# Pooled attention and two feed-forward layers: GpSimd takes other low parts in the first pair, and tile 11 in the others

## The chip, the cores and the metric

The kernel runs on one core of a Trainium2 chip. The metric is the device time of one execution in microseconds (us). A core has TensorE (PE; its weight loads are listed as PEld), VectorE (DVE), ScalarE (ACT), GpSimd (POOL) and SyncE (SP), which issues the DMAs here. Each engine works through its own queue in order; semaphores tie the queues together.

## The reference

Three stages follow one another. Attention over 4 batches and 8 heads, 1152 keys of 64 values; the queries are averaged by twos, so there are 576 of them. Then two feed-forward layers over 2304 tokens.

```python
q_pool = q.reshape(B, H, S // 2, 2, D).mean(axis=3)
scores = scale * np.matmul(q_pool, k.transpose(0, 1, 3, 2))
scores = scores - np.max(scores, axis=-1, keepdims=True)
attn = np.exp(scores)
attn = attn / (np.sum(attn, axis=-1, keepdims=True) + 1e-09)
x = np.matmul(attn, v)             # heads side by side: 2304 x 512
...
h = x @ w_in;  x = (h - np.tanh(h)) @ w_out
h = x @ w_in2; y = (h * (1.0 / (1.0 + np.exp(-1.702 * h)))) @ w_out2
```

## The kernel before

Matmuls run in a rounded format (fp32r). To keep fp32 accuracy an operand is split into a high part (a copy in fp32r) and a low part (the difference), and products of high and low parts are added up in PSUM. The low parts are subtractions with two inputs in SBUF; which engine makes them, VectorE or GpSimd, is what this change is about.

Heads go in pairs, 16 pairs. A pair has 18 tiles of 128 keys, nine for each of its heads; `g` counts tiles over all pairs and `g % 18` is called the tile's number below. For each tile the loop issues, in this order: `scores(g)` (four matmuls into one of two PSUM tiles `ps_sc`, then ScalarE's exponential `pf` and, for two tiles of three, a second one that gives the high part `ph`); one or two tiles of maxima for the next pair (`max_tile`: two matmuls and one reduction on VectorE, L327 and L331; their PSUM `ps_mx` has one buffer from tile 3 on); `rest(g - 1)`, the subtraction that gives the low part `pl` of the tile before (L457); `pv(g - 3)`, the products with V of the tile three back; and then what the tables `plan` and, for pair 0, `opening` list for this tile. An entry `(o, i)` runs in tile `i` for the pair `o` places further on. Tiles 1, 4, 7 of each head have no low part: there the full fp32 product is taken.

`pool_sub` says in which tiles the subtraction goes to GpSimd; all the others go to VectorE. `sum_q` makes `qs`, the pooled queries; `prep_qh` and `prep_ql` split them; `prep_kh` and `prep_kl` split K in two halves (L303 on ScalarE, L307 on GpSimd); `prep_v_split` splits V (L416, L419); `stack` copies the split parts by six DMAs into the layout for the scores (L315 to L320; L317 carries K's low part); `max_rows` turns the maxima of a head into the row that is subtracted (a small minimum L390 and a transpose L392 on VectorE). `kl` has one buffer: a new K low part can be written only when L317 of the pair before has read the old one. In pairs 8 to 14 weights of the first layer are converted beside attention, with steps on VectorE in tiles 6, 8, 11 and 15 (L138, L144, L151, L158) in five of these pairs.

Ahead of the loop stands the opening: loads, the splits of pair 0, and the maxima of its first head (`first_max`), which all must be known before the first exponential. `keep_warm` issues matmuls on zeros so that PE does not stand still, and `scores` issues some more in tiles 1 to 3. In PSUM, `ps_first` (two buffers of three banks) lies behind `ps_sc[0]`; when it closes, the second scores tile `ps_sc[1]` and `ps_two` (two buffers of maxima, up to tile 3) take its room.

Of the kernel before, what the change touches and what calls it, by code (L numbers as in the profile page):

```python
# [7 lines left out]
F32 = mybir.dt.float32  # L8
# [3 lines left out]
ALU = mybir.AluOpType  # L12
AX = mybir.AxisListType
# [15 lines left out]
def tile_pooled_attention_two_moe(  # L29
# [182 lines left out]
    def attention(ctx: ExitStack):  # L212
# [22 lines left out]
        def refill_v(i, n):  # L235
            old, new = [(*vt[x], vfs[x])[n] for x in (0, i)]
            nc.scalar.activation(new[:, :, D:128], old[:, :, D:128], AF.Copy)

        def refill_row(i):
            row = [stacks[x][1][D:D + 1, :] for x in (0, i)]  # L240
            nc.scalar.activation(row[1], row[0], AF.Copy)
# [21 lines left out]
        def load_k(p, rows=slice(0, 128)):  # L263
            if p not in kraw:
                kraw[p] = ap.tile([128, S], F32, tag="kr", name="kr", bufs=2)
            nc.sync.dma_start(out=kraw[p][rows], in_=k[p // NPB, p % NPB][rows])

        def load_v(p, s):
            vraw[p, s] = ap.tile([128, 2 * KG, D], F32, tag=f"vr{s}", name=f"vr{s}")
            nc.sync.dma_start(out=vraw[p, s], in_=v[p // NPB, p % NPB][:, s, 0:2 * KG])  # L270
# [11 lines left out]
        def sum_q(p, eng=nc.vector):  # L282
            eng.tensor_add(pairs[p]["qs"], qraw[p][:, 0], qraw[p][:, 1])
# [17 lines left out]
        def prep_kh(p, x):  # L301
            xs = slice(x * SP, (x + 1) * SP)
            nc.scalar.activation(pairs[p]["kh"][:, xs], kraw[p][:, xs], AF.Copy)  # L303
# [7 lines left out]
        def stack(p, s):  # L311
            d = pairs[p]
            a1, a2, q2, q3 = stacks[(2 * p + s) % 3]
            r = slice(64 * s, 64 * s + 64)
            nc.sync.dma_start(out=f32(a1[0:64, :]), in_=f32(d["kh"][r, :]))  # L315
            nc.sync.dma_start(out=f32(q2[0:64, :]), in_=f32(d["qh"][r, :]))
            nc.sync.dma_start(out=f32(a1[64:128, :]), in_=f32(d["kl"][r, :]))  # L317
            nc.sync.dma_start(out=f32(q2[64:128, :]), in_=f32(d["qh"][r, :]))
            nc.sync.dma_start(out=f32(a2[0:64, :]), in_=f32(d["kh"][r, :]))
            nc.sync.dma_start(out=f32(q3[0:64, :]), in_=f32(d["ql"][r, :]))  # L320
# [16 lines left out]
        def first_max(s, j, x, pool, parts, n, banks=2):  # L337
            d = pairs[0]
            a1, _, q2, _ = stacks[0]
            r = slice(64 * s, 64 * s + 64)  # L340
            lhs, rhs = (q2, a1) if s == 0 else (d["qh"], d["kh"])
            mx = pool.tile([128, banks, 512], F32, tag="mx", name="mx")
            if j < 4:
                for a in range(parts):
                    k0 = (x * parts + a) * n
                    nc.tensor.matmul(
                        mx[:, a, 0:n], lhs[r, 128 * j:128 * j + 128], rhs[r, k0:k0 + n],
                        start=True, stop=True)
            else:
                for a in range(parts):  # L350
                    for h in range(2):
                        q0, k0 = 512 + 64 * s - 64 * h, h * SP + a * n
                        nc.tensor.matmul(
                            mx[:, a, 0:n], bdqs[1][r, q0:q0 + 128], rhs[r, k0:k0 + n],
                            start=(h == 0), stop=(h == 1))
            c = 64 + 16 * x + 5 * s + j
            nc.vector.tensor_reduce(
                first_mt[:, c:c + 1], mx[:, 0:parts, 0:n], AX.XY, ALU.max, negate=True)

        def row_part(s, row, j):  # L360
            c = 5 * s + j
# [46 lines left out]
        def prep_v(p, s):  # L408
            prep_v_whole(p, s)
            prep_v_split(p, s)  # L410
# [12 lines left out]
        def scores(g):  # L423
            hd, t = divmod(g, KT)
            a1, a2, q2, q3 = stacks[hd % 3]
            pf = ap.tile([128, SP], F32, tag="pf", name="pf", bufs=5)
            ks = slice(128 * t, 128 * t + 128)
            sc = ps_sc[g % 2].tile([128, 2, 512], F32, tag="sc", name="sc")
            for x in range({1: 2, 2: 2, 3: 1}.get(g, 0)):
                nc.tensor.matmul(sc[:, x], *zeros, start=True, stop=True)  # L430
            for x in range(2):
                xs = slice(x * HB, (x + 1) * HB)
                nc.tensor.matmul(sc[:, x, 0:HB], a1[:, ks], q2[:, xs], start=True, stop=False)  # L433
                nc.tensor.matmul(sc[:, x, 0:HB], a2[:, ks], q3[:, xs], start=False, stop=True)  # L434

            def both(tile):
                return tile.rearrange("p (x i) -> p x i", x=2)

            nc.scalar.activation(both(pf), sc[:, :, 0:HB], AF.Exp, scale=SCALE)  # L439
            if whole(t):  # L440
                probs[g] = None, None, pf
                return
            ph = ap.tile([128, SP], F32R, tag="ph", name="ph", bufs=4)
            pl = ap.tile([128, SP], F32R, tag="pl", name="pl", bufs=3)
            if g in pool_cast:
                nc.gpsimd.tensor_scalar(
                    out=ph, in0=pf, scalar1=1.0, scalar2=1.0, op0=ALU.mult, op1=ALU.mult)
            else:
                nc.scalar.activation(both(ph), sc[:, :, 0:HB], AF.Exp, scale=SCALE)  # L449
            probs[g] = ph, pl, pf  # L450

        def rest(g):
            ph, pl, pf = probs[g]
            if ph is None:
                return
            eng = nc.gpsimd if g % NS in pool_sub.get(g // NS, (5, 14)) else nc.vector
            eng.tensor_tensor(pl, pf, f32(ph[:]), op=ALU.subtract)  # L457

        def pv(g):
# [76 lines left out]

        NS = 2 * KT
        LAG = 3
        pool_sub = {0: (5, 8, 11, 14, 17), NPAIR - 1: ()}
        pool_cast = [(NPAIR - 1) * NS + i for i in (3, 6, 9, 12)]  # L540
        early = {}
        when = (
# [46 lines left out]
        def q_low(out, r, hi):  # L589
            nc.gpsimd.tensor_tensor(out[r], d0["qs"][r], f32(hi[r]), op=ALU.subtract)  # L590
# [20 lines left out]
        q_corner(high, SP)  # L611
        refill_v(1, 0)
        ps_sc = [ctx.enter_context(tc.tile_pool(name="ps_sc0", bufs=1, space=PSUM))]
        with tc.tile_pool(name="ps_first", bufs=2, space=PSUM) as ps_first:
            warm = ps_sc[0].tile([128, 2, 512], F32, tag="sc", name="warm")

            def keep_warm(n, to=warm[:, 0]):
                for _ in range(n):
                    nc.tensor.matmul(to, *zeros, start=True, stop=True)

            keep_warm(11)
            for j in range(4):
                first_max(0, j, 0, ps_first, 3, 384, 3)
                keep_warm(2 if j < 3 else 1)
            first_max(0, 4, 0, ps_first, 2, HB, 3)
            keep_warm(2)
            first_row(0, flat(warm))
            copy_row(0, flat(warm))
            row = ps_first.tile([128, 3, 512], F32, tag="mx", name="row")
            keep_warm(1, row[:, 1])  # L630
            row_part(0, row[0:D + 1, 0, 0:128], 4)
            last_copy(0, row[:, 0, 0:128])
            first_max(1, 0, 0, ps_first, 3, 384, 3)
        new_pair(1)
        prep_kh(1, 0)
        prep_v_split(0, 0)
        k_low(d0["kl"], high, half(kraw[0], high, 0), d0["kh"], 0)
        k_low(d0["kl"], high, half(kraw[0], high, 1), d0["kh"], 1)
        q_low(d0["ql"], high, d0["qh"])
        load_q(1)  # L640
        sum_q(1, nc.gpsimd)
        stack(0, 1)
        prep_v(0, 1)
        load_v(1, 0)
        load_v(1, 1)
        load_k(2)
        ps_sc.append(ctx.enter_context(tc.tile_pool(name="ps_sc1", bufs=1, space=PSUM)))
        ps_two = ExitStack()
        ps_mx = ps_two.enter_context(tc.tile_pool(name="ps_two", bufs=2, space=PSUM))

        total = NPAIR * NS
        max_at = {}
        for h, g in zip(range(2, 9), (1, 1, 1, 2, 2, 3, 4), strict=True):
            max_at.setdefault(g, []).append(
                lambda h=h: first_max(1, h // 2, h % 2, ps_mx, 2, HB))
        max_at[5] = [second_row]
        for n in range(1, NPAIR):
            for h in range(2 * QJ):
# [12 lines left out]
            (3, 9): [(load_k,)], (3, 17): [(prep_qs,)],  # L671
        }
        opening = {
            (0, 1): [(lambda p: prep_kh(1, 1),)], (0, 5): [(lambda p: refill_v(1, 1),)],
            (1, 3): [(prep_bdq, 0)], (0, 4): [(lambda p: refill_row(1),)],
            (0, 7): [(lambda p: refill_v(1, 2),),
                     (lambda p: nc.gpsimd.memset(f32(bdqs[0][:, 0:288]), 0.0),)],
            (0, 9): [(lambda p: fill(2),)],
            (1, 4): [(prep_kl, 0)], (1, 5): [(prep_kl, 1)], (2, 9): [(prep_qs, nc.gpsimd)],
            (2, 1): [(load_q,)], (1, 6): [(prep_qh,), (prep_ql, nc.gpsimd)],  # L680
            (1, 7): [(prep_bdq, 1), (stack, 0)], (1, 8): [(prep_v, 0)], (1, 10): [(stack, 1)],
            (1, 12): [(prep_v_split, 1)], (1, 13): [(max_rows, 0)], (1, 15): [(prep_v_whole, 1)],
            (2, 10): [(prep_qh,)], (2, 11): [(prep_bdq, 0)],
            (2, 12): [(prep_bdq, 1)], (2, 13): [(prep_kh, 0), (load_v, 0)],
# [289 lines left out]
```

## Time and profile before

| | |
|---|---|
| timed runs | 1305.17, 1300.92, 1301.36 us; median 1301.36 |
| profiled execution | 1305.66 us, of which the span from the first to the last instruction is 1303.9 |
| busy in the span | PE 1292.7, VectorE 986.1, ScalarE 754.0, GpSimd 361.6 us |
| mean granted clock of PE | 0.995 of full speed |

Attention takes about the first 500 us, the two layers the rest. The times in the rows below count from the span's start. In a timeline a row reads: start, duration, engine, line of the kernel, operation, output <- inputs, shapes, count, and in brackets how long the engine had been idle and what ended that.

### The profile page before, as it was taken

Reading aid. Unit: us, or ns where it says so; the run is one execution under the profiler, and the core shown is the slowest. Engines: PE = TensorE matmul, PEld = TensorE weight load, DVE = VectorE, ACT = ScalarE, POOL = GpSimd, SP = SyncE. Lnnn points to the kernel's source line nnn. Section 1 sums busy time; section 2 is a strip of 40 time slices with the busy share of each in tenths; the row PEclk is TensorE's granted clock in tenths of the full one; section 3 lists DMA queues with packets and bytes.
Section 4 is the critical chain, followed back from the end, with each engine's and each line's share of the span. In section 5 each row is a group of like instructions: output and inputs, shape, how many; then the busy total and the mean of one; then the engine's idle time right before and its main releaser. Section 6 shows DMA issues by size and latency. Waiting matters only on the chain.

```text
span 1303.9 us, 18915 instructions
## 1 busy us (share of the span) xinstructions
PE 1292.7 (99%) x7043; PEld 1155.5 (89%) x7043; DVE 986.1 (76%) x1277; ACT 754.0 (58%) x1159; POOL 361.6 (28%) x277
## 2 busy tenths in 40 slices
PE   9999999999999999999999999999999999999998
PEld 6899999999999999889889889889889889889887
DVE  5777777888879888999999999999944645645433
ACT  5777777777777767787666665665543322322211
POOL 6633333344334323224332332332100100100000
PEclk7999999999999999999999999999999999999999
DMA  7666666766767531211111111111211111111012
GB/s 189 169 152 160 180 172 162 171 170 167 186 170 181 136 95 35 60 46 50 50 33 49 49 33 46 36 33 50 65 35 47 49 33 50 49 33 33 25 41 80
DMA packets 58739, 116.25 MB, mean 89 GB/s; under 512 B 24856, under 2 KB 28952, under 8 KB 58648
## 3 DMA queue, kind: packets, MB, share of 16 engines
q1 hardware_dynamic: 58648, 115.05, 33.9%
q8 instruction: 55, 0.90, 0.3%
q14 instruction: 36, 0.29, 0.1%
HBM read 66.58 MB, written 4.79 MB: 55 GB/s over the span
## 4 chain that ended last, share of the span: by engine, by line
PE 76%; DVE 13%; ACT 6%; issue 2%; POOL 1%; DMA 1%; DVEq 0%; SPq 0%; POOLq 0%; ACTq 0%
PE y L850 21%; PE h L755 20%; PE pv L479 11%; PE pv L469 7%; PE sc L434 6%; PE sc L433 5%; PE mx L327 5%; DVE gg L813 2%; DVE gg L796 2%; ACT u L794 2%; DVE wt L144 1%; DVE wt L138 1%; DVE xb L870 1%; DVE wt L158 1%; ACT a L815 1%
## 5 line engine op out<-in xcount | busy, mean ns | idle before, releaser
L331 DVE TENSOR_REDUCE mt<-mx 128x1 fp32r<-128x576 f32 x270 | 203.6, 754 | 83.3 <-PE mx L327 78.9
L439 ACT ACTIVATE pf<-sc 128x576 f32<-128x576 f32 x288 | 188.5, 655 | 127.9 <-PE sc L434 117.5
L755 PE MATMUL h<-hl,big 128*128 128x512 f32 (+1 forms) x940 | 211.6, 377 | 0.0
L755 PEld LDWEIGHTS h<-hl,big 128*128 128x128 f32 x940 | 174.0, 188 | 28.6
L850 PE MATMUL y<-g,big 128*128 128x512 f32 (+1 forms) x780 | 185.3, 368 | 1.5 <-POOL g L767 1.3
L433 PE MATMUL sc<-q,big 128*128 128x288 f32 x576 | 184.5, 333 | 0.1
L850 PE MATMUL y<-big,g 128*128 128x512 f32 x702 | 181.0, 390 | 0.0
L166 POOL TENSOR_TENSOR big<-wt,big 128x512 fp32r<-128x512 f32 x46 | 61.4, 1334 | 379.7 <-ACT big L165 379.7
L434 PE MATMUL sc<-q,a 65*128 65x288 f32 x576 | 164.8, 300 | 0.0
L850 PEld LDWEIGHTS y<-g,big 128*128 128x128 f32 x780 | 142.6, 188 | 21.5 <-POOL g L767 3.1
L765 ACT ACTIVATE g<-gg 128x1024 fp32r<-128x1024 f32 (+1 forms) x80 | 78.0, 975 | 138.5 <-DVE gg L826 76.3
L850 PEld LDWEIGHTS y<-big,g 128*128 128x128 f32 x702 | 131.6, 188 | 27.1
L479 PE MATMUL pv<-ph,big 128*128 128x288 f32 x768 | 142.5, 296 | 0.9 <-ACT u L485 0.9
L870 DVE TENSOR_TENSOR xb<-xb,y 128x512 f32<-128x512 f32 (+1 forms) x114 | 72.1, 655 | 86.7 <-PE y L850 86.7
L457 DVE TENSOR_TENSOR pl<-pf,ph 128x576 fp32r<-128x576 f32 x159 | 132.7, 835 | 2.2 <-ACT ph L449 1.5
L755 PE MATMUL h<-hl,w 128*128 128x512 f32 (+1 forms) x564 | 127.0, 377 | 0.0
L449 ACT ACTIVATE ph<-sc 128x576 fp32r<-128x576 f32 x188 | 122.8, 653 | 0.0
L755 PEld LDWEIGHTS h<-hl,w 128*128 128x128 f32 x564 | 104.4, 188 | 17.1
L327 PE MATMUL mx<-kh,big 128*128 128x288 f32 x540 | 117.9, 300 | 1.0 <-DVE mt L331 0.6
L479 PEld LDWEIGHTS pv<-ph,big 128*128 128x128 f32 x768 | 116.7, 189 | 1.7 <-issue 0.7
L433 PEld LDWEIGHTS sc<-q,big 128*128 128x128 f32 x576 | 110.5, 192 | 5.9 <-ACT ph L449 0.5
L815 ACT ACTIVATE a<-u 128x1024 f32<-128x1024 f32 (+1 forms) x40 | 39.1, 978 | 132.3 <-DVE gg L813 132.3
(126 smaller groups left out, 2225.4 us busy)
## 6 DMA issues: line engine op xcount, KB each, us to landing
raw<-in_moe_w_in_dram SPq DMA_DIRECT2D x32, 512.0 KB
raw<-in_moe_w_out_dram SPq DMA_DIRECT2D x32, 512.0 KB
big<-kh SPq DMA_DIRECT2D x31, 288.0 KB
q<-qh SPq DMA_DIRECT2D x62, 144.0 KB
big<-kl SPq DMA_DIRECT2D x31, 288.0 KB
a<-kh SPq DMA_DIRECT2D x31, 288.0 KB
kr<-in_k_dram SPq DMA_DIRECT2D x15, 576.0 KB
qr<-in_q_dram SPq DMA_DIRECT2D x15, 576.0 KB
```

The lines of the kernel that those rows point to most:

```text
L327: nc.tensor.matmul(mx[:, a, 0:n], bdqs[p % 2][:, 128 * j:128 * j + 128], d["kh"][:, k0:k0 + n], start=True, stop=True)
L331: nc.vector.tensor_reduce(d["mt"][:, c:c + 1], mx[:, :, 0:n], AX.XY, ALU.max, negate=True)
L433: nc.tensor.matmul(sc[:, x, 0:HB], a1[:, ks], q2[:, xs], start=True, stop=False)
L434: nc.tensor.matmul(sc[:, x, 0:HB], a2[:, ks], q3[:, xs], start=False, stop=True)
L439: nc.scalar.activation(both(pf), sc[:, :, 0:HB], AF.Exp, scale=SCALE)
L449: nc.scalar.activation(both(ph), sc[:, :, 0:HB], AF.Exp, scale=SCALE)
L457: eng.tensor_tensor(pl, pf, f32(ph[:]), op=ALU.subtract)
L469: nc.tensor.matmul(accs[hd][x], vfs[hd % 3][:, t // 3, :], pf[:, x * HB:(x + 1) * HB], start=False, stop=False)
L479: nc.tensor.matmul(accs[hd][x], w[:, t, :], r[:, x * HB:(x + 1) * HB], start=(t == 0 and n == 0), stop=(t == KT - 1 and n == 2))
L755: nc.tensor.matmul(hb[:, j, 0:TBS[b]], wi[:, c, w, :], x[r][c], start=(k == 0), stop=(k == 3 * NKC - 1))
L850: nc.tensor.matmul(ys[m][:, 0:w], lhsT, rhs, start=(fp == 0 and not low and j == p == 0), stop=(fp == 1 and low and j == 1))
L870: nc.vector.tensor_add(dst, dst, ys[m][:, 0:w])
```

## The change

Four things. In the opening, `ps_first` becomes two pools of one buffer each, `first_max` takes one of them by the parity of `s + j`, and its reduction is handed back as a function, so that the matmuls of the second head's first maxima are issued ahead of the last part of the first head's row, and their reduction behind that row. In pair 0 the subtractions of tiles 0, 2 and 3 go to GpSimd too, and other low parts (`q_low`, `sum_q`, `prep_v`, pair 1's `prep_kl`) move behind them into the loop, with the DMAs that follow them. Maxima of the second head are spread differently over tiles 1 to 4, and one matmul on zeros goes. In pairs 1 to 14, GpSimd's second subtraction is that of tile 11 and no longer that of tile 14.

```diff
@@ first_max
+            if banks == 3:
+                pool = pool[(s + j) % 2]
...
-            nc.vector.tensor_reduce(
-                first_mt[:, c:c + 1], mx[:, 0:parts, 0:n], AX.XY, ALU.max, negate=True)
+            def reduce():
+                nc.vector.tensor_reduce(
+                    first_mt[:, c:c + 1], mx[:, 0:parts, 0:n], AX.XY, ALU.max, negate=True)
+
+            return reduce
@@ scores
-            for x in range({1: 2, 2: 2, 3: 1}.get(g, 0)):
+            for x in range({1: 2, 2: 1, 3: 1}.get(g, 0)):
@@ rest
-            eng = nc.gpsimd if g % NS in pool_sub.get(g // NS, (5, 14)) else nc.vector
+            eng = nc.gpsimd if g % NS in pool_sub.get(g // NS, (5, 11)) else nc.vector
@@
-        pool_sub = {0: (5, 8, 11, 14, 17), NPAIR - 1: ()}
+        pool_sub = {0: (0, 2, 3, 5, 8, 11, 14, 17), NPAIR - 1: ()}
@@ the opening
-        with tc.tile_pool(name="ps_first", bufs=2, space=PSUM) as ps_first:
+        with tc.tile_pool(name="ps_first0", bufs=1, space=PSUM) as first0, \
+                tc.tile_pool(name="ps_first1", bufs=1, space=PSUM) as first1:
+            ps_first = first0, first1
...
-                first_max(0, j, 0, ps_first, 3, 384, 3)
-                keep_warm(2 if j < 3 else 1)
-            first_max(0, 4, 0, ps_first, 2, HB, 3)
+                first_max(0, j, 0, ps_first, 3, 384, 3)()
+                keep_warm(2)
+            first_max(0, 4, 0, ps_first, 2, HB, 3)()
...
-            row = ps_first.tile([128, 3, 512], F32, tag="mx", name="row")
-            keep_warm(1, row[:, 1])
+            other = first_max(1, 0, 0, ps_first, 3, 384, 3)
+            row = first0.tile([128, 3, 512], F32, tag="mx", name="row")
             row_part(0, row[0:D + 1, 0, 0:128], 4)
             last_copy(0, row[:, 0, 0:128])
-            first_max(1, 0, 0, ps_first, 3, 384, 3)
+            other()
...
-        q_low(d0["ql"], high, d0["qh"])
         load_q(1)
-        sum_q(1, nc.gpsimd)
-        stack(0, 1)
-        prep_v(0, 1)
-        load_v(1, 0)
-        load_v(1, 1)
-        load_k(2)
...
-        for h, g in zip(range(2, 9), (1, 1, 1, 2, 2, 3, 4), strict=True):
+        for h, g in zip(range(2, 9), (1, 1, 2, 2, 3, 3, 4), strict=True):
@@ the table opening
-            (0, 1): [(lambda p: prep_kh(1, 1),)], (0, 5): [(lambda p: refill_v(1, 1),)],
-            (1, 3): [(prep_bdq, 0)], (0, 4): [(lambda p: refill_row(1),)],
+            (0, 1): [(lambda p: prep_kh(1, 1),), (lambda p: q_low(d0["ql"], high, d0["qh"]),),
+                     (stack, 1), (lambda p: load_v(1, 0),), (lambda p: load_k(2),)],
+            (0, 3): [(lambda p: sum_q(1, nc.gpsimd),)], (0, 5): [(lambda p: refill_v(1, 1),)],
+            (1, 3): [(prep_bdq, 0)], 
+            (0, 4): [(lambda p: refill_row(1),), (prep_v, 1), (lambda p: load_v(1, 1),)],
...
-            (1, 4): [(prep_kl, 0)], (1, 5): [(prep_kl, 1)], (2, 9): [(prep_qs, nc.gpsimd)],
-            (2, 1): [(load_q,)], (1, 6): [(prep_qh,), (prep_ql, nc.gpsimd)],
-            (1, 7): [(prep_bdq, 1), (stack, 0)], (1, 8): [(prep_v, 0)], (1, 10): [(stack, 1)],
+            (2, 9): [(prep_qs, nc.gpsimd)], (2, 1): [(load_q,)],
+            (1, 6): [(prep_qh,), (prep_kl, 0), (prep_kl, 1), (prep_ql, nc.gpsimd)],
+            (1, 7): [(prep_bdq, 1)], (1, 8): [(stack, 0)], (1, 9): [(prep_v, 0)],
+            (1, 10): [(stack, 1)],
```

## Rows read from the trace of the kernel before

**Rows 1.** The page, busy time of each engine over the span: PE and PEld

```profile
PE 1292.7 (99%) x7043; PEld 1155.5 (89%) x7043; DVE 986.1 (76%) x1277; ACT 754.0 (58%) x1159; POOL 361.6 (28%) x277
```

**Rows 2.** Table by stage: stretch, length, busy time (count) per engine, PE clock, DMA

```profile
0.00:17.50 17.50, 15.02 (x61) 10.28 (x61) 11.93 (x16) 11.29 (x18) 15.80 (x20) 1.00 0.74 196
17.50:31.20 13.70, 13.70 (x47) 11.03 (x46) 6.12 (x10) 5.23 (x8) 5.88 (x5) 0.50 0.79 199
```

**Rows 3.** PE's waits from 9 to 60 us: total, times, longest

```profile
PE sc L430 <- DVE big L357: 0.7, 1, 0.7
...
PE mx L346 <- DVE big L357: 0.6, 1, 0.6
```

**Rows 4.** Timelines of PE and ACT near the end of the opening

```profile
31.97 0.29 PE L433 MATMUL sc<-q,big 128*128 128x288 f32 x1
...
46.05 0.53 PE L479 MATMUL pv<-ph,big 128*128 128x288 f32 x2 [0.36 <-ACT u L485]
...
43.93 0.69 ACT L290 ACTIVATE qh<-qs 128x576 fp32r<-128x576 f32 x1 [2.93 <-DMA q<-qh]
...
45.59 0.71 ACT L485 ACTIVATE u<-pv 128x288 f32<-128x288 f32 x2
```

**Rows 5.** Timeline of GpSimd in the opening

```profile
13.03 2.77 POOL L586 TENSOR_TENSOR kl<-kr,kh 64x576 fp32r<-64x576 f32 x2
...
31.99 1.42 POOL L457 TENSOR_TENSOR pl<-pf,ph 128x576 fp32r<-128x576 f32 x1 [8.52 <-ACT ph L449]
35.09 1.43 POOL L294 TENSOR_TENSOR ql<-qs,qh 128x576 fp32r<-128x576 f32 x1 [1.68 <-ACT qh L290]
...
36.76 0.75 POOL L416 TENSOR_SCALAR big<-vr 128x384 fp32r<-128x384 f32 x1
...
38.55 1.43 POOL L457 TENSOR_TENSOR pl<-pf,ph 128x576 fp32r<-128x576 f32 x1
40.04 1.05 POOL L245 MEMSET a<- 1x1152 f32 x1
...
42.41 1.49 POOL L283 TENSOR_TENSOR qs<-qr 128x576 f32<-128x576 f32 x1
```

**Rows 6.** Timelines of VectorE, then GpSimd, tiles 13 to 17 of pair 4

```profile
168.33 0.75 DVE L457 TENSOR_TENSOR pl<-pf,ph 128x576 fp32r<-128x576 f32 x1
...
170.18 0.75 DVE L294 TENSOR_TENSOR ql<-qs,qh 128x576 fp32r<-128x576 f32 x1
...
172.62 0.76 DVE L331 TENSOR_REDUCE mt<-mx 128x1 fp32r<-128x576 f32 x1 [0.83 <-PE mx L327]
173.30 0.91 DVE L457 TENSOR_TENSOR pl<-pf,ph 128x576 fp32r<-128x576 f32 x1
...
172.17 3.33 POOL L307 TENSOR_TENSOR kl<-kr,kh 128x576 fp32r<-128x576 f32 x2
```

**Rows 7.** Timelines in pair 15; last, VectorE's group of L144 in pairs 1 to 14

```profile
485.38 0.74 DVE L457 TENSOR_TENSOR pl<-pf,ph 128x576 fp32r<-128x576 f32 x1
486.05 1.75 DVE L144 SCALAR_TENSOR_TENSOR wt<-raw,wt 128x512 int32<-128x512 int32 x1
...
485.40 1.86 POOL L166 TENSOR_TENSOR big<-wt,big 128x512 fp32r<-128x512 f32 x1 [0.69 <-ACT big L165]
...
L144 DVE SCALAR_TENSOR_TENSOR wt<-raw,wt 128x512 int32<-128x512 int32 x5 | 3.2, 631 | 0.0
```

**Rows 8.** Timeline of VectorE, tiles 15 and 16 of pair 12

```profile
411.30 1.20 DVE L158 SCALAR_TENSOR_TENSOR wt<-raw,wt 128x512 int32<-128x512 int32 x1
412.43 0.74 DVE L331 TENSOR_REDUCE mt<-mx 128x1 fp32r<-128x576 f32 x1
```

**Rows 9.** Table by stage, pair 4; last two columns: DMA busy share, GB/s

```profile
168.00:169.00 1.00, 1.00 (x8) 0.90 (x7) 1.00 (x3) 0.03 (x1) 0.00 (x0) 1.00 1.05 235
169.00:170.00 1.00, 1.00 (x9) 1.00 (x9) 0.86 (x4) 0.84 (x2) 0.00 (x0) 1.00 0.68 145
170.00:171.00 1.00, 1.00 (x10) 1.00 (x9) 0.92 (x2) 0.59 (x2) 0.57 (x1) 1.00 0.32 95
171.00:172.00 1.00, 1.00 (x9) 1.00 (x9) 0.76 (x1) 0.96 (x2) 1.00 (x1) 1.00 0.19 54
```

More of the change, by code (lines that the diff above doesn't have):

```diff
@@ L652, in attention @@
         max_at = {}
-        for h, g in zip(range(2, 9), (1, 1, 1, 2, 2, 3, 4), strict=True):
+        for h, g in zip(range(2, 9), (1, 1, 2, 2, 3, 3, 4), strict=True):
             max_at.setdefault(g, []).append(
-                lambda h=h: first_max(1, h // 2, h % 2, ps_mx, 2, HB))
+                lambda h=h: first_max(1, h // 2, h % 2, ps_mx, 2, HB)())
         max_at[5] = [second_row]
```

## The prediction

> **What bounds the kernel now.** I read the page's engine table first: TensorE is busy for 99% of the span [rows 1], so a change is worth only the time in which TensorE stands still, runs at the lower clock, or does work that disappears. Then the stages. The table by stage shows that the first 17.5 us and the 13.7 us behind them are the only poor ones: PE does 15.02 us of work in 17.5, and from 17.5 to 31.2 it is busy all the time at a granted clock of 0.50, that is 1.2 GHz instead of 2.4 [rows 2]. Ahead of the fall PE had two waits for VectorE, 0.7 us for the PSUM of tile 1's scores and 0.6 us for a buffer of maxima [rows 3]. The reader is to see there a price: 13.7 us at half clock is 6.85 us of lost PE work.
>
> Next I followed what PE waits for once the clock is back. The first product of head 1 stands at 46.05 and waits for ScalarE's copy `u` (45.59); ScalarE in turn had been held until 43.93 by `qh` of pair 2 [rows 4], and the timeline of GpSimd shows the reason: `qs` of pair 2 begins at 42.41 and takes 1.49, so it ends at 43.90 [rows 5]. So at the end of the opening GpSimd's queue sets the time, not PE. From pair 1 on PE has practically no waits; there VectorE's order around the 14 pairs' tiles matters only if it makes a maximum late.
>
> The profiled execution took 1305.66 us. Of the three timed runs one took 1305.17 and two 1300.92 and 1301.36; the distance of 4.3 us is what a half-clock stretch of this size would leave after GpSimd's queue has eaten part of its 6.85. I read the median as a run without that stretch, and work the sum against the profiled 1305.66.
>
> **Opening, PE and VectorE.** The two one-buffer pools let the first matmuls of head 1's maxima stand ahead of the row's last part; tile 1's scores then lie over the pool whose last reader is a short row copy and not the 1.36 us reduction. The 0.7 us wait goes. One max job moves from tile 1 to tile 2 and one from tile 2 to 3, and the subtractions of tiles 0, 2 and 3 (0.75 us each on VectorE) leave VectorE, so the 0.6 us wait shrinks to some 0.25. One zero matmul fewer is 0.3 us less work. With less idling ahead of 17.5 I expect the full clock to stay. Tile 6, which started at 31.97 [rows 4], then starts at 31.97 - 6.85 - 1.3 = 23.8, to some 25 if small waits come back.
>
> **Opening, GpSimd.** Its queue gets three subtractions more and, with them, the order: low part of K (2.77 for two halves, from 13.03), subtraction 0, `ql`, subtraction 2, `qs` of pair 1, subtraction 3, V split of head 1, subtraction 5, K low of pair 1, its `ql`, a short memset, subtraction 8, the fills, V split, `qs` of pair 2. Prices by start to start [rows 5]: K low 2.75; each subtraction, `ql` or `qs` 1.4 (the subtraction at 38.55 has 1.43); V split 1.8 (36.76 to 38.55); fills 2.4 (40.04 to 42.41); memset 0.3. In order: 2.75 + 5 x 1.4 + 1.8 + 1.4 + 2.75 + 1.4 + 0.3 + 1.4 + 2.4 + 1.8 + 1.5 = 24.5. It has no idle time any more (before: 8.5 us in front of subtraction 5 and 1.7 in front of `ql` [rows 5]), because its inputs are ready earlier than it is. So `qs` of pair 2 ends at 13.0 + 24.5 = 37.5, up to 38.9 if VectorE's subtractions 6 and 9 get in between (0.7 each); I take 37.8. That is 6.1 us ahead of 43.90. ScalarE and PE follow with the same 2.15 us (43.90 to 46.05), so head 1's first product stands at 40.0. PE's own pace would bring it there earlier, since from tile 6 to that product it took 14.1 us with all waits, and is at some 37: PE waits about 3 us for GpSimd. The opening therefore gives 6.1 us (5.0 to 6.4) against the profiled execution, 1305.66 - 6.1 = 1299.6, but almost nothing against a run that kept its clock.
>
> The stack of `qs`, `qh` and K low of pair 1 goes to SP one tile later than before, behind `load_q` of pair 2, which now waits for `qs` of pair 1 at some 21.4. It costs nothing: its last transfer is issued near 31.5, and head 2 starts six tiles after head 1's first product at 40.
>
> **Tile 11 instead of 14, pairs 1 to 14.** By busy time nothing changes: VectorE gives up tile 11's subtraction and takes tile 14's, 0.75 us each, and behind tile 14 VectorE stood idle 0.83 us ahead of tile 16's reduction [rows 6]. But GpSimd's order changes: before, K low of the next pair but one had to wait behind subtraction 14 (it starts at 172.17 [rows 6]); now GpSimd is through with subtraction 11 and the V split at some 168.4, and K low runs as soon as the transfer that reads the old K low has landed.
>
> What that does is read from [rows 6]: the subtraction of tile 15 that begins at 173.30, in the middle of K low's first half, takes 0.91 instead of 0.75, and K low takes 3.33 for the two halves instead of 2.77. The two engines do not share, they take turns by whole instructions. [Rows 7] show the turn: a VectorE subtraction at 485.38, GpSimd's at 485.40 (1.86 us), and VectorE's next two-operand instruction right behind at 486.05 lasts 1.75 where its mean elsewhere is 0.63: GpSimd, which had been waiting, went in between. The reductions, which read PSUM, are not stretched. The Trainium skill, SBUF — State Buffer, section Who interferes with whom, says the same: one port pair is shared, a VectorE instruction with two SBUF inputs and a GpSimd instruction that reads SBUF exclude each other, and the loser waits for the whole instruction. By that rule, with which the trace agrees, it is not enough to count busy time.
>
> When may K low start? The transfer of the old K low is followed by three more of 432 KB together. In pair 4 the DMA traffic ends at 172 [rows 9]. Taken evenly, 432 KB back from there is 168.4 (54 + 95 + 145 + part of 235); for an engine that is still busy at the end, its sixteenth (27 KB at 235/16 KB per us) is 1.8 us, so 170.2. The slowest engine decides, so I take 170.2 or a little later.
>
> - Ordinary pair (nine of them: 1 to 7, 9, 11): `ql` at 170.18 goes first, K low's first half holds until 172.2, subtraction 14 runs 172.2 to 172.9, tile 16's reduction starts 0.25 late, subtraction 15 waits for the second half, tile 17's reduction is 0.4 late. A reduction may be about 0.25 late before PE waits. So 0.1 us, up to 0.7 where the landing falls badly: 0.2 x 9 = 1.8.
> - Pairs with a weight conversion in tile 15 (8, 10, 12, 13; 14 has one too, but no K low behind it): tile 15's conversion step, 1.20 before because it already had to wait its turn [rows 8], some 0.65 alone, now follows subtraction 14 without a reduction between them. Subtraction 14 waits for K low's first half (in pair 12 to 412.2, then to 412.9), K low's second half goes ahead of the conversion (to 414.2), the conversion ends at 414.8, and tile 16's reduction, which stood at 412.43, starts there. PE then waits 2.0 us; 1.5 if K low starts some tenths earlier. Where it starts so early that the row of maxima's small minimum is the one held up, the sum is 1.5 as well. I take 1.6 less the 0.3 that these pairs already lose: 1.3 x 4 = 5.2.
>
> Sum: 1299.6 + 1.8 + 5.2 = 1306.6, and as the runs that kept their clock lie at 1301.1 and not at 1299.6, half a microsecond more: 1307.
>
> **The rivals.** *The turns cost nothing* (not slower). It hangs on one point: whether K low's first half starts behind tile 14's reduction and away from the conversion. If it starts near 172 or later, as it did before, subtraction 14 falls into the idle 0.83 us. For it: VectorE has slack in every ordinary pair. Against it: nothing holds K low back any more. Time: 1299.6 to 1302.
>
> *K low starts at 168.4 in all pairs.* Then it gets its turn behind subtraction 12, the row's minimum is held 1.3 us, the next reduction comes 1.35 late, and with `ql` a pair loses 1.27: 13 x 1.27 = 16.5, so 1316. Against it: the tail of the traffic [rows 9].
>
> *The clock falls at the new wait.* PE would idle 3 us near 38, longer than the waits ahead of 17.5. Another 13.7 us at half clock would cost up to 6.85: with the other losses some 1312.
>
> *GpSimd isn't last.* If PE reached head 1 unhindered, 3 us more would come back: 1296.5 without the turns, faster. Against it: the 24.5 us of work without a gap.
>
> **How the numbers follow.** My forecast has 0.47, the turns costing nothing 0.30, K low early everywhere 0.10, the clock 0.07, GpSimd not last 0.06. A measurement of this kernel tells about 0.3% from no change, 1297.5 to 1305.3. Of the forecast's 0.47 some 0.08 lies below 1305.3. Slower: 0.39 + 0.10 + 0.07 = 0.56; same: 0.08 + 0.30 = 0.38; faster 0.06. The range from 1299.5 to 1313 leaves out the early K low, part of the last rival and some tails. The forecast's own range is 1303 to 1312.
>
> **What would show it.** Right: full clock from 17 to 31; GpSimd without a gap from 13 to some 38; ScalarE's `qh` of pair 2 right behind it and PE waiting there; in the pairs, K low some 1 to 2 us earlier against the tiles, and PE waits behind reductions of tiles 16 and 17 in pairs 8, 10, 12 and 13, of 1 to 2 us each. Wrong: pairs in which VectorE's reductions start no later against the tiles than before, or a half-clock stretch near 40.

## The result and the profile after

The change made the kernel slower. The median of four runs is 1312.99 us (1311.37 to 1314.05) against 1301.72 us of before (four runs, 1300.92 to 1305.17): a ratio of 1.0085 with a 95% interval of 1.0068 to 1.0101, or 11.3 us. The forecast was 1307.0, so the sign and the places were right and the size was too small. The profiled execution took 1314.05 us with a span of 1312.2; that of before, which took longer than any of its four runs (1305.66), had 1303.9.

The page's engine line of the kernel after answers to [rows 1]. TensorE (PE) is busy for only 1.2 us more; the span has grown by 8.3:

```profile
PE 1293.9 (99%) x7042; PEld 1155.5 (88%) x7042; DVE 987.5 (75%) x1274; ACT 754.2 (57%) x1159; POOL 357.2 (27%) x280
```

The table by stage of the kernel after (columns as in [rows 2]: stretch, length, busy time of PE, PEld, VectorE, ScalarE, GpSimd, granted clock, DMA share, GB/s), for the two stretches of [rows 2], the one behind them, and two that lie inside later stages:

```profile
0.00:17.50 17.50, 16.44 (x63) 11.43 (x64) 11.63 (x16) 11.18 (x18) 15.25 (x19) 1.00 0.74 195
17.50:31.20 13.70, 13.13 (x80) 10.91 (x80) 7.33 (x11) 10.57 (x19) 12.15 (x11) 1.00 0.75 208
31.20:46.00 14.80, 12.14 (x64) 10.48 (x64) 6.89 (x11) 8.90 (x16) 11.22 (x13) 0.83 0.84 200
...
40.90:47.70 6.80, 5.83 (x20) 5.26 (x21) 1.71 (x4) 4.85 (x10) 2.90 (x3) 0.51 0.51 144
...
296.90:300.30 3.40, 3.40 (x17) 3.40 (x16) 2.74 (x4) 1.19 (x2) 0.91 (x1) 0.51 0.93 202
```

The stretch from 17.5 to 31.2, at half clock before, is now at full clock, and the count of PE's matmuls in it is 80 instead of 47. But two new stretches at half clock have come: 6.8 us from 40.9, of which PE was busy for 5.83 (2.9 us of PE work lost), and 3.4 us from 296.9, in pair 8 (1.7 lost). The first begins within a wait of PE and the second 0.9 us behind one, as the rows on PE's waits and the timelines below show. The first row is from the window 9 to 60 us, which [rows 3] shows for before; the second is from 60 to 500 us, where the same view of the kernel before lists one wait, of 0.5 us. Columns: what waited, for what, total us, times, longest:

```profile
PE pv L485 <- ACT u L491: 1.9, 1, 1.9
...
PE mx L327 <- DVE mt L331: 6.2, 8, 1.8
```

The first is the predicted wait at head 1's first product, the second the predicted one for VectorE's reductions. Timelines of GpSimd, ScalarE and PE follow the first back, as [rows 4, 5] did:

```profile
16.53 1.42 POOL L463 TENSOR_TENSOR pl<-pf,ph 128x576 fp32r<-128x576 f32 x1 [0.58 <-ACT ph L455]
...
26.56 1.42 POOL L463 TENSOR_TENSOR pl<-pf,ph 128x576 fp32r<-128x576 f32 x1 [1.31 <-ACT ph L455]
...
38.31 1.41 POOL L283 TENSOR_TENSOR qs<-qr 128x576 f32<-128x576 f32 x1
...
39.75 0.68 ACT L290 ACTIVATE qh<-qs 128x576 fp32r<-128x576 f32 x1 [4.50 <-POOL qs L283]
...
41.41 0.71 ACT L491 ACTIVATE u<-pv 128x288 f32<-128x288 f32 x2
...
41.87 0.85 PE L485 MATMUL pv<-ph,big 128*128 128x288 f32 x2 [1.90 <-ACT u L491]
```

`qs` of pair 2 ends at 39.72, `qh` follows at once, `u` behind it, and PE stands for 1.90 us until 41.87. That is 4.2 us ahead of the 46.05 of before [rows 4]; of these the half clock behind it takes back most (2.75), so that pair 1's first exponential starts at 54.65 instead of 56.08.

Where the rest went is seen by pairs. This table is worked out from the timeline of ScalarE: the distance in us from one pair's first exponential to the next pair's.

```
pair       1     2     3     4     5     6     7     8     9    10    11    12    13    14
before  30.22 29.83 29.83 29.83 29.82 29.83 29.83 29.84 30.39 29.84 30.20 29.84 30.25 29.95
after   29.99 30.55 30.20 29.83 29.88 30.02 30.92 32.64 30.64 31.42 30.86 30.91 31.13 29.88
```

Pairs 2 to 13 lose 9.7 us: 6.3 in pairs 8, 10, 12 and 13, which convert weights in tile 15, 1.8 in pairs 7 and 11, and 1.6 in the other six. Three kinds of turn make these losses; they differ in which instruction of VectorE K low holds up. The timelines of VectorE, GpSimd and PE in pair 8 show the one that was predicted for these pairs, those in pair 7 the second, and those in pair 10 the third:

```profile
291.89 1.64 DVE L463 TENSOR_TENSOR pl<-pf,ph 128x576 fp32r<-128x576 f32 x1
293.45 1.89 DVE L158 SCALAR_TENSOR_TENSOR wt<-raw,wt 128x512 int32<-128x512 int32 x1
295.27 0.75 DVE L331 TENSOR_REDUCE mt<-mx 128x1 fp32r<-128x576 f32 x1
...
291.49 3.31 POOL L307 TENSOR_TENSOR kl<-kr,kh 128x576 fp32r<-128x576 f32 x2 [2.69 <-DMA big<-kl]
...
296.07 0.53 PE L327 MATMUL mx<-kh,big 128*128 128x288 f32 x2 [1.79 <-DVE mt L331]
...
258.20 1.40 DVE L396 TENSOR_TENSOR mt<-mt 128x5 fp32r<-128x5 f32 x1
259.63 0.21 DVE L398 STREAM_TRANSPOSE tt<-mt 128x32 f32<-128x32 f32 x1
259.95 0.76 DVE L331 TENSOR_REDUCE mt<-mx 128x1 fp32r<-128x576 f32 x1
...
258.12 2.81 POOL L307 TENSOR_TENSOR kl<-kr,kh 128x576 fp32r<-128x576 f32 x2 [0.47 <-DMA big<-kl]
...
353.80 1.76 DVE L294 TENSOR_TENSOR ql<-qs,qh 128x576 fp32r<-128x576 f32 x1
...
353.53 3.31 POOL L307 TENSOR_TENSOR kl<-kr,kh 128x576 fp32r<-128x576 f32 x2 [1.44 <-DMA big<-kl]
```

In pair 8, K low starts as soon as the transfer of the old one has landed, 2.15 us behind the row's minimum (289.34). VectorE's subtraction 14 waits for the first half (1.64 instead of 0.75), the conversion waits for the second (1.89 instead of 1.20, [rows 8]), and the reduction of tile 16 begins only at 295.27: PE waits 1.79. In pair 7 the transfer lands earlier, K low starts 0.08 us ahead of the row's minimum, and that instruction of 128x5 values, which takes 0.15 elsewhere, lasts 1.40. Everything behind it on VectorE is late by 1.25. Pairs 11 and 13 show the same (1.40 and 1.39 for the minimum). In pair 10, K low starts 0.90 us behind the minimum and 0.27 ahead of `ql`, which then takes 1.76 instead of 0.75; pairs 2, 3 and 12 show the same (1.77, 1.42 and 1.26 for `ql`), and the conversion of pairs 10, 12 and 13 is not stretched (0.68).

What the change released is plain from one distance. In the kernel before, K low starts 3.18 or 3.19 us behind the row's minimum in every pair from 1 to 13, because subtraction 14 holds it there; after the change it starts anywhere from 0.58 us ahead of the minimum to 3.07 behind it, according to when the transfer of the old K low lands.

### The profile page after: what moved, and what is told of

It is laid out like the page before. It is cut to its first block, busy times and chain, and to the rows that moved or that the text cites. A ratio compares the mean times of both kernels' runs of the same rounds, so it can differ in the third digit from the quotient of the medians.

```text
span 1312.2 us, 18922 instructions
## 1 busy us (share of the span) xinstructions
PE 1293.9 (99%) x7042; PEld 1155.5 (88%) x7042; DVE 987.5 (75%) x1274; ACT 754.2 (57%) x1159; POOL 357.2 (27%) x280
## 4 chain that ended last, share of the span: by engine, by line
PE 75%; DVE 16%; ACT 6%; issue 2%; POOL 1%; DVEq 0%; ACTq 0%
PE y L855 21%; PE h L760 20%; PE pv L485 11%; PE pv L475 6%; PE mx L327 6%; PE sc L440 5%; PE sc L439 5%; DVE gg L818 3%; DVE gg L801 2%; ACT u L799 2%; DVE wt L144 2%; ACT a L820 1%; DVE wt L138 1%; DVE wt L158 1%; DVE xb L875 1%
```

## The experiments

The experiments are counted in the order in which they stand. K low, `ql`, `qs`, the minimum and the tiles are named as in the section on the kernel before.

**Tile 11 instead of 14 alone, in the opening of before.**

```diff
-            eng = nc.gpsimd if g % NS in pool_sub.get(g // NS, (5, 14)) else nc.vector
+            eng = nc.gpsimd if g % NS in pool_sub.get(g // NS, (5, 11)) else nc.vector
```

> The kernel before with one edit: GpSimd's second subtraction in tile 11 instead of 14 in pairs 1 to 14. Turns (VectorE and GpSimd exclude each other by whole instructions, and K low now starts among VectorE's dense tiles 13 to 16): pairs 2 to 13 lose 7 to 9 us together, most of it in pairs 8, 10, 12 and 13, so 1308.5 to 1310.5 against 1301.7. Opening (the loss came from the opening and its half-clock stretches, the move of a tile is free): 1301 to 1303.

Measured: 1312.29 us, median of 6 (1307.88 to 1315.57), against 1302.44; ratio 1.0066 (1.0047 to 1.0085). This one number accounts for the whole loss of the change within the spread of the runs (1312.29 against 1312.99), and the time lies above the bracket of the theory of turns. PE's waits from 60 to 500 us, then VectorE and GpSimd in pair 12:

```profile
PE mx L327 <- DVE mt L331: 6.0, 8, 1.4
```

```profile
415.35 0.75 DVE L294 TENSOR_TENSOR ql<-qs,qh 128x576 fp32r<-128x576 f32 x1
416.06 0.76 DVE L331 TENSOR_REDUCE mt<-mx 128x1 fp32r<-128x576 f32 x1
416.73 1.27 DVE L457 TENSOR_TENSOR pl<-pf,ph 128x576 fp32r<-128x576 f32 x1
417.93 1.90 DVE L158 SCALAR_TENSOR_TENSOR wt<-raw,wt 128x512 int32<-128x512 int32 x1
419.75 0.74 DVE L331 TENSOR_REDUCE mt<-mx 128x1 fp32r<-128x576 f32 x1
...
415.85 3.43 POOL L307 TENSOR_TENSOR kl<-kr,kh 128x576 fp32r<-128x576 f32 x2 [2.21 <-DMA big<-kl]
```

This is the sequence of the forecast for pair 12, step by step: `ql`, K low's first half, subtraction 14, K low's second half, the conversion, and then the late reduction. Of the four pairs with a conversion it is the only one here; in pair 8 `ql` is held (1.99) and in pairs 10 and 13 the minimum (1.39 each). Pairs 8, 10, 12 and 13 lose 5.9 us (31.63, 31.26, 31.63, 31.13), the others of pairs 2 to 13 together 2.5. These 8.3 us lie in the expected 7 to 9; the time does not lie in its bracket, and the paragraph on what stays open comes back to that.

**The opening alone**: all of the change but for that line, which keeps `(5, 14)`.

> The changed kernel with tile 14 put back for tile 11: the opening part alone. Turns: pairs 2 to 13 are as long as before (29.8 us, the four with a conversion 30.2 to 30.4); the opening alone gives what its wait for GpSimd and the clock leave, 0 to 3 us slower than before: 1301.5 to 1304.5. Opening: 1310 to 1313.

Measured: 1302.81 us, median of 12 (1301.40 to 1304.36), ratio 0.9999 (0.9988 to 1.0010). The opening is worth nothing that can be measured. Pairs 2 to 13 are as long as before (29.81 to 29.85, and 30.21 to 30.23 in pairs 9, 11 and 13). Pair 1 took 31.13 in the profiled execution (30.22 before): at its end PE waited 1.06 us, by the profile for a transfer. `qs` of pair 2 runs 37.33 to 38.74, the wait at `u` is there with 1.9 us, and the table by stage shows the clock behind it:

```profile
17.50:31.20 13.70, 13.14 (x82) 11.16 (x82) 7.78 (x11) 11.02 (x19) 12.69 (x11) 1.00 0.81 220
...
41.40:44.80 3.40, 3.40 (x14) 3.04 (x13) 1.13 (x2) 3.33 (x6) 2.10 (x3) 0.52 0.68 201
```

**K low without its reads**: the first experiment, and K low written by a memset from pair 2 on.

```diff
+            if p >= 2:
+                nc.gpsimd.memset(f32(pairs[p]["kl"][:, xs]), 0.0)
+                return
             nc.gpsimd.tensor_tensor(
```

> The first experiment's kernel, but from pair 2 on K's low part is filled with zeros by a memset of the same shape, which reads nothing, in place of the subtraction; the low part of K is left out there. Turns: nothing is left that shuts VectorE out in tiles 13 to 17, so pairs 2 to 13 come to 29.8 to 29.9 us each and the time to 1301 or less. Order (VectorE is late merely because tile 14's subtraction now stands directly ahead of the conversion step, whatever GpSimd does): pairs 8, 10, 12, 13 stay 0.9 us or more above 29.9, and the time 1306 or more.

Measured: 1299.11 us in one run, span 1297.3. Pairs 1 to 14 take 29.77 to 30.04 us. VectorE and GpSimd in pair 8, then in pair 3:

```profile
284.22 0.75 DVE L294 TENSOR_TENSOR ql<-qs,qh 128x576 fp32r<-128x576 f32 x1
284.92 0.76 DVE L334 TENSOR_REDUCE mt<-mx 128x1 fp32r<-128x576 f32 x1
285.60 0.75 DVE L460 TENSOR_TENSOR pl<-pf,ph 128x576 fp32r<-128x576 f32 x1
286.26 0.68 DVE L158 SCALAR_TENSOR_TENSOR wt<-raw,wt 128x512 int32<-128x512 int32 x1
...
283.93 1.10 POOL L308 MEMSET kl<- 128x576 f32 x2 [1.43 <-DMA big<-kl]
...
133.47 0.16 DVE L393 TENSOR_TENSOR mt<-mt 128x5 fp32r<-128x5 f32 x1
...
133.39 1.10 POOL L308 MEMSET kl<- 128x576 f32 x2 [0.46 <-DMA big<-kl]
```

The order of instructions is that of the change, every VectorE instruction has its short duration (the conversion 0.68, which answers to the estimate of 0.65), and the loss is gone. So the loss is not the order on VectorE but the two-input K low on GpSimd. The memset is also shorter than the subtraction, 1.10 us for 2.8, but its length does not explain it: in pair 8 it overlaps `ql`, which keeps its 0.75, and in pair 3 it starts 0.08 us ahead of the minimum, just as K low did in pair 7 of the changed kernel, and the minimum takes 0.16 and not 1.40. The Trainium skill, SBUF — State Buffer, section Who interferes with whom, has this distinction too: a VectorE instruction with two SBUF inputs collides with a GpSimd instruction that reads SBUF, not with one that only writes. The trace agrees on both halves (0.75 here; subtraction 14 took 1.64 beside the reading K low).

This run is of use for the opening too. It has the opening of before, and its clock stayed at full speed in that execution:

```profile
17.50:31.20 13.70, 13.29 (x82) 11.22 (x82) 10.02 (x14) 10.45 (x17) 8.74 (x8) 1.00 0.79 204
...
37.13 1.47 POOL L283 TENSOR_TENSOR qs<-qr 128x576 f32<-128x576 f32 x1
```

Its `qs` of pair 2 ended at 38.60, where the changed opening alone had 38.74, and head 1's first product stood at 40.75 against 40.88. PE came to it with a wait of 0.35 us instead of 1.91, and no half clock followed, so pair 1 began at 50.78 and not at 52.51. Without the half clock the old opening is as quick as the new one up to that product, and 1.7 us ahead behind it in these two executions.

**The conversion's last step moved** from tile 15 to tile 12, on top of the first experiment.

```diff
-            ("i", 0, (-8, 0), (-8, 6), (-8, 8), (-8, 11), (-8, 15), (-8, 17)),
+            ("i", 0, (-8, 0), (-8, 6), (-8, 8), (-8, 11), (-8, 12), (-8, 17)),
...
```

> The first experiment's kernel with the conversion's last VectorE step in tile 12, where tile 11's subtraction has gone, instead of tile 15. Turns: no two two-operand instructions stand back to back in tile 15 any more; pairs 8, 10, 12, 13 lose 0.1 to 0.7 us instead of 0.9 to 2.8, so 1303 to 1306. Opening: no difference to the first experiment.

Measured: 1308.88 us, median of 6 (1305.99 to 1312.18), ratio 1.0048 (1.0031 to 1.0066): a miss. The median is 3.4 us below that of the first experiment, but the two ranges overlap. Pair 8, VectorE and GpSimd:

```profile
283.40 1.41 DVE L457 TENSOR_TENSOR pl<-pf,ph 128x576 fp32r<-128x576 f32 x1
284.73 0.15 DVE L390 TENSOR_TENSOR mt<-mt 128x5 fp32r<-128x5 f32 x1
...
285.90 1.77 DVE L294 TENSOR_TENSOR ql<-qs,qh 128x576 fp32r<-128x576 f32 x1
287.60 0.74 DVE L331 TENSOR_REDUCE mt<-mx 128x1 fp32r<-128x576 f32 x1
...
283.18 1.01 POOL L419 TENSOR_TENSOR big<-vr,big 128x384 fp32r<-128x384 f32 x1
285.63 3.32 POOL L307 TENSOR_TENSOR kl<-kr,kh 128x576 fp32r<-128x576 f32 x2 [1.44 <-DMA big<-kl]
```

In tile 12 the conversion pushes VectorE's subtraction 12 behind GpSimd's V split (1.41 for 0.75), and K low, which starts 0.27 us ahead of `ql`, holds that for 1.77. So the turn moved to another place. Pairs 8, 10, 12 and 13 still take 31.51, 30.55, 31.32 and 31.57 us, a loss of 5.2 where the first experiment had 5.9. In the eight ordinary pairs, which this edit does not touch, 2.5 us of loss there became none here, so most of the difference that the pairs of the two profiled executions show comes from where K low happened to start. The conversion's neighbourhood in tile 15 is thus not the only place where K low costs.

**Three subtractions**: tiles 5, 11 and 14 on GpSimd, in the opening of before.

```diff
-            eng = nc.gpsimd if g % NS in pool_sub.get(g // NS, (5, 14)) else nc.vector
+            eng = nc.gpsimd if g % NS in pool_sub.get(g // NS, (5, 11, 14)) else nc.vector
```

> The kernel before with GpSimd's subtractions in tiles 5, 11 and 14 of pairs 1 to 14: tile 11 is added, tile 14 stays. Turns: subtraction 14 holds K low back as before, so pairs 2 to 13 stay at 29.8 to 29.9 us (30.4 or less in 8, 10, 12, 13); time within 2 us of the kernel before. The move of tile 11 by itself (its subtraction delays the V split and all behind it on GpSimd): about 1310, as in the first experiment.

Measured: 1302.19 us, median of 11 (1300.84 to 1307.20), against 1302.06; ratio 1.0001 (0.9987 to 1.0015). Tile 11 on GpSimd costs nothing as long as subtraction 14 stands ahead of K low. GpSimd in pair 8:

```profile
284.83 1.98 POOL L457 TENSOR_TENSOR pl<-pf,ph 128x576 fp32r<-128x576 f32 x1 [1.77 <-ACT ph L449]
286.78 3.76 POOL L307 TENSOR_TENSOR kl<-kr,kh 128x576 fp32r<-128x576 f32 x2
```

K low waits behind subtraction 14 here, and the pairs are as long as before (29.83 to 29.89, and 30.22 to 30.28 in pairs 9, 11 and 13). GpSimd has a third subtraction in each pair and VectorE one less, and neither changes the time: what counts is that K low starts behind tile 14, here again 3.17 to 3.19 us behind the minimum in every pair.

**`qs` of pair 2 one tile earlier**, in the opening of before.

```diff
-            ... (2, 9): [(prep_qs, nc.gpsimd)],
+            ... (2, 8): [(prep_qs, nc.gpsimd)],
```

> The kernel before with one edit: the pooled queries of pair 2 are made in tile 8 of pair 0 instead of tile 9, which puts them ahead of subtraction 8 and the fills in GpSimd's queue. GpSimd sets the end of the opening: ScalarE is no longer held for qh of pair 2, head 1's first product comes 2 to 3 us earlier, 1298.5 to 1300.5 against 1302.4. PE or something else sets it: no difference.

Measured: 1300.17 us, median of 12, ratio 0.9996 (0.9984 to 1.0009): no difference by the interval. The runs lie in two groups, eight at 1299.45 to 1300.48 and four at 1303.84 to 1305.22; those of before do as well (24 at 1300.37 to 1303.12 and 11 at 1305.22 to 1306.38). The mean granted clock of a run goes with its group: 0.999 or more in the lower one, 0.994 to 0.997 in the upper. The profiled execution is one of the upper group, with half clock in a part of this stretch:

```profile
17.50:31.20 13.70, 12.52 (x56) 10.23 (x56) 7.69 (x12) 6.84 (x11) 6.21 (x6) 0.75 0.76 197
```

So the old opening meets half clock in some executions and not in others. Taken by themselves, a comparison made only after the result, the runs at full clock have a median of 1299.95 with the edit and of 1301.46 before, 1.5 us less.

**The new opening with `qs` one tile earlier**: the second experiment with the same edit. And **the same with three subtractions**, `(5, 11, 14)`.

> The second experiment's kernel (new opening, tile 14) with the pooled queries of pair 2 in tile 8 as well. GpSimd sets the end of the opening: PE no longer stands still near 40, the half-clock stretch behind it goes, and the new opening's earlier tiles are kept: head 1's first product near 38, 3 to 4 us less, 1298 to 1300 against 1302.8. Otherwise no difference.

In the next one, "the third line here" is the kernel just described.

> The kernel of the third line here with GpSimd's subtractions in tiles 5, 11 and 14. Turns: K low is held behind subtraction 14 and VectorE has one subtraction less, so the pairs are as long as before or 0.3 us shorter in 8, 10, 12 and 13: 1297 to 1300, the fastest of all. If tile 11 on GpSimd costs by itself: 1306 or more.

Measured: 1300.30 us, median of 11 (1299.07 to 1301.00), ratio 0.9980 (0.9969 to 0.9991), and 1300.28 us, median of 12 (1298.18 to 1302.36), ratio 0.9984 (0.9974 to 0.9995). Both are faster than before by some 0.2%, 0.3 us above what was expected. One is as good as the other, so the pairs gained nothing from the third subtraction. GpSimd and the stage of the first of them:

```profile
33.03 1.41 POOL L283 TENSOR_TENSOR qs<-qr 128x576 f32<-128x576 f32 x1
```

```profile
31.20:46.00 14.80, 14.06 (x93) 12.62 (x92) 9.66 (x16) 11.93 (x22) 12.81 (x15) 1.00 0.87 203
```

`qs` runs at 33.03, ahead of a subtraction, the fills and a V split; the wait at `u` between 9 and 60 us is gone, PE does 14.06 us of work in the stretch instead of 12.14, at full clock, and pair 1 starts at 50.01 (54.65 in the changed kernel, 52.51 in the second experiment). The old opening with this edit came as low in eight of its twelve runs, but had the four at 1303.84 to 1305.22; here none of the eleven lies above 1301.00, and the mean clock is 0.999 or more in all 23 runs of the two kernels. So neither part gains alone beyond its interval: the edit brings the time, and the new opening, whose wait it takes away, keeps the early half clock away.

## Why the prediction was right and wrong

**The two parts apart.** The working came to 1300.1 for the opening (1299.6 and the half microsecond) and 7.0 for the pairs. The second experiment measures the first at 1302.8, and the change's median less that gives 10.2 for the pairs. The two errors, 2.7 and 3.2, have one sign and make up the miss. One microsecond of the first was in the sum itself: the working says that the opening gives almost nothing against a run that kept its clock, and puts such runs at 1301.1, but it adds half a microsecond to 1299.6 and not the whole 1.5.

**What bounds the opening: right.** The full clock from 17.5 to 31.2, GpSimd's queue as the bound, and ScalarE and PE behind it with the same 2.15 us (39.72 to 41.87) are all in the rows. PE's wait of 0.7 us is gone and that of 0.6 is 0.2. That the opening gives almost nothing against a run that kept its clock was said, and the second and third experiments show it. PE waited 1.9 us and not about 3; by the forecast's own numbers, tile 6 at 23.8 and 14.1 us from there, it would have come to the product at 37.9 and waited 2.1.

**GpSimd's 24.5 us without a gap: the step that failed in the opening.** The prices held in sum (`ql` of pair 1 took 0.5 us more than its 1.4, the two V splits 0.2 less each), the gaps did not. GpSimd stood 0.58 us ahead of subtraction 0 and 1.31 ahead of subtraction 5, waiting for ScalarE's `ph`: 1.9 together, and the predicted 37.8 plus 1.9 is the measured 39.7. In the second experiment the gaps were 0.8 us. I had taken it that all its inputs were ready earlier than it is. The first exponential itself stood at 15.20 instead of 13.95 in this execution. It lies between 13.95 and 14.91 in the executions profiled with the old opening and between 14.23 and 15.36 with the new one. One microsecond of the 1.25 comes from the very start: the eleven matmuls on zeros there, the same in both kernels, took 5.06 us in this execution and 4.03 in that of before, so the change isn't shown to cause that part.

**The clock at the new wait: a rival that I priced at 0.07 and that came.** I expected PE to idle there and still did not carry its price into the sum. A half-clock stretch near 40 was also one of its own signs of being wrong. The half clock lasted 6.8 us in the profiled execution and 3.4 in that of the second experiment, 2.9 and 1.7 us of PE work, and another 1.7 in pair 8. Not the full 13.7 us that the rival assumed; but with the later `qs` it is the reason why the profiled opening gained 1.4 us by pair 1's first exponential and not 6.1. The last two experiments, which remove the wait, keep the clock in all 23 runs.

**Tile 11 instead of 14: right in mechanism.** That busy time says nothing here, that K low no longer has subtraction 14 ahead of it, that engines take turns by whole instructions, and which instructions lose: the traces show each step, and three experiments separate it from its rivals. Without the change's line there is no loss (second), without K low's reads none (third), and with K low held back none (fifth). The rival that the turns cost nothing hung on K low starting near 172 of pair 4 or later. In pair 4 itself it started at 170.30, which is 170.9 by the times of before, as the pair began 0.6 us earlier, and it cost nothing; in most of the others it did cost.

**The price of the turns: the step that was mis-sized.** Conversion pairs: 1.3 each forecast, 5.2 in all; 6.3 measured, of which 1.7 is the half clock of pair 8, and 5.9 in the first experiment, without a fall there. The size of this term was good to 15%, but partly by luck. The sequence that it was reckoned from, with the conversion held, came in one of the four pairs (8 here, 12 in the first experiment); in the others `ql` or the minimum was held, the latter a case that the working had also priced, at 1.5. And the 0.3 "that these pairs already lose" was read wrongly: before, pairs 8, 10 and 12 take 29.84 like the ordinary ones, and it is 9, 11 and 13 that take 0.4 to 0.6 more. PE's waits were also not all of 1 to 2 us: 1.8 in pair 8 and 1.0 in pair 13, but some 0.5 at a time in pairs 10 and 12. Ordinary pairs: 0.2 each for nine, 1.8; in the eight of them from 2 on, 3.3 were measured here and 2.5 in the first experiment. The 0.2 came from one landing time, that of pair 4, and the old K low's landing against the row's minimum varies from pair to pair: K low starts from 0.6 us ahead of the minimum to 3.1 behind it. The reckoning of that landing had a slip too: by the profile's sizes the three transfers behind L317 carry 144, 288 and 144 KB, which is 576 and not 432. The same working then gives some 169.6 instead of 170.2, ahead of `ql` at 170.18 and not behind it, and `ql` held up is what pairs 2, 3, 10 and 12 show. In pairs 7, 11 and 13 the landing falls so early that the minimum loses the turn, and these are the 1.09, 0.66 and 0.88 us. That was the rival "K low starts at 168.4 in all pairs", right in its mechanism, its price of the right order (1.27 forecast each) and wrong in "all": the cases that I set against each other as alternatives occur side by side in one execution. I should have priced a mixture.

**What stays open.** The medians give 9.9 us for the pairs in the old opening and 10.2 in the new one; the pairs of the two profiled executions add up to 8.3 and 9.7. The recorded clocks say something on the rest: of the six runs of the first experiment the two with a mean clock of 1.000 took 1307.88 and 1310.89 us, and the four at 0.994 to 0.998 took 1311.61 to 1315.57. Against 1301.81, the median of the runs of before at full clock beside them, those two are 6 and 9 us slower by the turns alone, and what lies above goes along with half clock, in the opening or in a pair; where it fell is known for the profiled execution alone. Why the landings vary by more than 3 us was not tried.

## What to carry to other kernels

Before an instruction is moved between two engines that shut each other out, look at what it was holding back: here 0.75 us of work moved in each pair and nothing else, and the instruction that it had kept in its place cost 10 us over the pairs. A start that hangs on a DMA's landing has to be priced over all the places where it may land, not at the one that the timeline of a single pair shows. And at the end of an opening, first ask whose output the next stage waits for (here one `qs`), and put that ahead in its queue; the rearrangement gained nothing measurable without it and 0.2% with it.

## What the runs showed of the hardware that was not expected

The smallest instruction pays the full turn: the minimum of 128x5 values went from 0.15 to 1.40 us when GpSimd's half of K low had started 0.08 us before it. Between two GpSimd instructions that stand back to back a waiting VectorE instruction gets in, and between two of VectorE's a waiting one of GpSimd's, so that two VectorE instructions in a row can each be stretched by nearly a whole GpSimd instruction (1.64 and 1.89 us for 0.75 and 0.68). And a wait can cost twice: 0.9 us behind PE's wait of 1.79 us in pair 8 the granted clock fell to 0.51 for 3.4 us, with PE busy all the time, another 1.7 us lost. Of the eight waits of that row it was the longest, and the only one with such a stretch behind it.
